# Reordering k conversions, two O units and one attention pair in a fused retention and feed-forward kernel

## The chip, the cores and the metric

One core of a Trainium2 chip. The metric is the time of one execution in microseconds (us), median over executions; lower is better. Each execution also has a span, from the first instruction of the program to the last, which the profiler gives to 0.1 us. All executions told here were in the fast state, except one of the kernel before (span 208.7 us), which is left out of every figure but the medians that the runs list and the count of 44 below. A ratio is the mean time of one kernel's fast runs over that of the kernel before's fast runs in the same rounds, so it is not quite the ratio of the medians that stand beside it.

## The reference

```python
def _attn_ref(q, k, v):                      # q, k, v: (4, 8, 768, 64)
    gamma = 1.0 - 2.0 ** (-5.0 - np.arange(H))
    for t in range(S):
        state = gamma * state + einsum('bhd,bhe->bhde', k[:, :, t], v[:, :, t])
        y[:, :, t] = scale * einsum('bhd,bhde->bhe', q[:, :, t], state)
def _moe_ref(x, w_in, w_out):                # x: y as (3072, 512)
    h = x @ w_in                             # (3072, 2048)
    return (h * np.cos(h)) @ w_out           # (3072, 512)
```

The sequence is cut into chunks of 128 steps. Twelve "pairs" (two batch entries, one chunk) go through attention; every two pairs make a group of 512 tokens that then goes through the two large products.

## The kernel before

Names used below: **A** is the score product of a pair (TensorE), masked by VectorE; **Y** is its output product, copied to `xt` by ScalarE, followed by **S**, the state product; **F** is a block of the first large product, ending in a cosine on ScalarE and a product on VectorE; **O** units (four matmuls) make the second large product. Pairs count from 0, so the "fourth pair" is pair 3 and the "seventh" pair 6. F (2,2) and F (3,0) are blocks of pairs 2 and 3 (`pair_f`); in the second half of the program F runs over whole groups, and F (2,11) is unit 11 of group 2. k is converted to bf16 by ScalarE (`conv_k`), q and v are converted by GpSimd (POOL), which also issues the loads. The program is one fixed order for each engine:

```python
    def conv_k(p, on_act, bs=(0, 1)):
        for b in bs:
            if on_act:
                nc.scalar.copy(out=qk[p % NB][:, b, 1], in_=kf[SLOT[p]][b])
    ...
    def act(bank, out):
        nc.scalar.activation(out=cb, in_=bank, func=AF.Sin, bias=halfpi)
        ...
        nc.vector.tensor_tensor(out=out, in0=bank, in1=cb, op=ALU.mult)
    ...
    cq(3)
    stage_t_dma(3)
    cv(3)
    load_both(("k", 4), ("q", 4), ("k", 5), ("q", 5), ("v", 4), ("v", 5))
    ...
    pair_f(2, 0)
    conv_k(4, True)
    pair_f(2, 1)
    attend(3)
    cq(4)
    stage_t_dma(4)
    pair_f(2, 2)
    conv_k(5, True)
    cq(5)
    ...
    pair_f(2, 3)
    stage_y(3, nc.scalar.copy)
    unit_o(1, 0, 0)
    pair_f(3, 0)
```

Seven PSUM banks rotate among A, Y, F and O. Which bank each takes is fixed when the program is built, by a small model of the engines' clocks.

## Time and profile before

| | before |
|---|---|
| median time, first three runs | 207.13 us |
| profiled execution: time, span | 207.53 us, 205.7 us |
| TensorE busy | 196.7 us, 96% |
| next engine (ACT) | 114.4 us, 56% |

How to read a line of the timeline: start, length, engine, source line, operation, output and input, number of merged instructions, and in brackets how long the engine had stood idle and what ended that. The lines themselves are in the prediction.

### The profile page before, as it was taken

The page shows a single profiled execution, that of the slowest core. Times are in us where ns is not written, and L with a number is a line of the kernel's source. Part 1 is how long each engine was busy: PE and PEld are TensorE (multiplying, and loading weights), DVE is VectorE, ACT ScalarE, POOL GpSimd, SP SyncE. Part 2 cuts the span into 40 slices and gives each one's busy share as a digit, 9 for nine tenths or more (in the row PEclk, how much of TensorE's full clock was granted, in tenths as well). Part 3 has the DMA queues.
Part 4 walks back from the last instruction along what each step waited for, and adds up shares of the span by engine and source line. Part 5 has one row for each costly group of instructions (what it writes and reads, how often), then busy time and mean ns, then how long its engine had stood idle before and what let it go on. Part 6 is the DMA issues. An engine that isn't in the chain of part 4 may idle for free.

```text
span 205.7 us, 4083 instructions
## 1 busy us (share of the span) xinstructions
PE 196.7 (96%) x1609; PEld 112.4 (55%) x1631; DVE 113.0 (55%) x190; ACT 114.4 (56%) x192; POOL 91.3 (44%) x98
## 2 busy tenths in 40 slices
PE   6789999999899999999999999999999999999993
PEld 2468544558797555556454466444465444444453
DVE  4886872723958545679784366844467233444000
ACT  7796862277885736597446466453554654553120
POOL 8998238399699659979931730000000000000000
PEclk9999999999999999999999999999999999999999
DMA  6999999959999995999999905101101101110212
GB/s 157 351 246 205 218 247 288 329 121 275 328 134 246 333 217 112 291 319 185 255 371 362 255 29 127 53 5 49 51 3 53 51 14 40 51 51 4 99 51 102
DMA packets 33571, 34.34 MB, mean 167 GB/s; under 512 B 23376, under 2 KB 25680, under 8 KB 33552
## 3 DMA queue, kind: packets, MB, share of 16 engines
q0 software_dynamic: 7824, 22.29, 38.9%
q1 hardware_dynamic: 24544, 11.44, 24.2%
q10 hardware_dynamic: 1184, 0.36, 0.7%
q8 instruction: 12, 0.20, 0.4%
q14 instruction: 7, 0.06, 0.1%
HBM read 27.26 MB, written 6.29 MB: 163 GB/s over the span
## 4 chain that ended last, share of the span: by engine, by line
PE 89%; DMA 2%; POOL 2%; DVE 2%; issue 2%; ACT 2%; ACTq 0%; POOLq 0%; DVEq 0%
PE bank L388 38%; PE bank L342 32%; PE bank L353 7%; PE bank L283 3%; PE bank L261 2%; DMA vf<-in_v_dram 2%; PE bank L288 2%; PE bank L366 2%; PE bank L408 2%; PE st_ps L305 1%; POOL qf L130 1%; DVE am L270 1%; ACT cosb L331 1%; POOL kf L137 1%; PE bank L232 0%
## 5 line engine op out<-in xcount | busy, mean ns | idle before, releaser
L335 DVE TENSOR_TENSOR gt<-bank,cosb 128x512 bf16<-128x512 f32 x96 | 65.0, 689 | 61.2 <-ACT cosb L331 61.0
L331 ACT ACTIVATE cosb<-bank,halfpi 128x512 bf16<-128x512 f32 x96 | 65.0, 688 | 51.1 <-PE bank L342 43.0
L388 PE MATMUL bank<-w_out_sb,gt 128*128 128x512 bf16 x357 | 88.2, 379 | 1.0 <-issue 0.5
L342 PE MATMUL bank<-xt,w_in 128*128 128x512 bf16 x294 | 74.1, 380 | 0.7 <-issue 0.4
L388 PEld LDWEIGHTS <-gt 128*128 128x128 bf16 x368 | 35.4, 98 | 41.0
L342 PEld LDWEIGHTS <-w_in 128*128 128x128 bf16 x304 | 33.7, 114 | 30.8
L270 DVE TENSOR_TENSOR am<-bank,mask 128x512 bf16<-128x512 f32 x48 | 30.4, 682 | 4.0 <-PE bank L261 3.9
L204 POOL TENSOR_TENSOR vs<-vf,gk 128x512 bf16<-128x512 f32 x21 | 21.4, 1042 | 10.3 <-DMA vf<-in_v_dram 8.8
L197 POOL TENSOR_TENSOR qk<-qf,gq 128x512 bf16<-128x512 f32 x18 | 18.4, 1040 | 9.6 <-DMA qf<-in_q_dram 3.1
L210 ACT CAST qk<-kf 128x512 bf16<-128x512 f32 x24 | 13.9, 618 | 14.1 <-DMA kf<-in_k_dram 13.9
L395 ACT COPY ob<-bank 128x512 f32<-128x512 f32 x23 | 13.4, 585 | 12.9 <-PE bank L388 12.6
L292 ACT CAST xt<-bank 128x512 bf16<-128x512 f32 x24 | 12.8, 591 | 5.9 <-PE bank L288 5.8
L353 PE MATMUL bank<-xt,w_in 128*128 128x256 bf16 x128 | 14.6, 273 | 0.8 <-DVE gt L335 0.7
L353 PEld LDWEIGHTS <-w_in 128*128 128x128 bf16 x128 | 13.9, 113 | 1.7 <-issue 1.2
L317 DVE CAST stb<-st_ps 64x512 bf16<-64x512 f32 x14 | 9.6, 686 | 3.6 <-PE st_ps L305 3.4
L288 PE MATMUL bank<-am,vs 128*64 128x128 bf16 x192 | 11.4, 220 | 0.0
L283 PEld LDWEIGHTS <-stb 128*64 128x64 bf16 x160 | 8.8, 109 | 4.0 <-issue 3.1
L283 PE MATMUL bank<-qkt,stb 128*64 128x128 bf16 x160 | 10.5, 222 | 0.3 <-ACT stb L317 0.3
L137 POOL DMA_DIRECT2D kf<-in_k_dram x9 | 10.5, 1168 | 0.0
L288 PEld LDWEIGHTS <-vs 128*64 128x64 bf16 x192 | 9.9, 110 | 0.5 <-issue 0.4
L137 POOL DMA_DIRECT2D qf<-in_q_dram x8 | 9.2, 1152 | 0.0
L137 POOL DMA_DIRECT2D vf<-in_v_dram x8 | 9.2, 1150 | 0.0
(47 smaller groups left out, 95.2 us busy)
## 6 DMA issues: line engine op xcount, KB each, us to landing
out_dram<-ob SPq DMA_DIRECT2D x23, 256.0 KB, 2.3
kf<-in_k_dram POOLq DMA_DIRECT2D x9, 512.0 KB, 6.1
qf<-in_q_dram POOLq DMA_DIRECT2D x8, 512.0 KB, 7.2
vf<-in_v_dram POOLq DMA_DIRECT2D x8, 512.0 KB, 8.2
vf<-in_v_dram POOLq DMA_DIRECT2D x8, 256.0 KB, 5.3
w_out_sb<-in_moe_w_out_dram POOLq DMA_DIRECT2D x4, 512.0 KB, 12.5
qf<-in_q_dram POOLq DMA_DIRECT2D x6, 256.0 KB, 7.1
w_in<-in_moe_w_in_dram POOLq DMA_DIRECT2D x3, 512.0 KB, 8.3
```

What stands on the lines that cost most here:

```text
L137: nc.gpsimd.dma_start(out=both[n][SLOT[p]].rearrange("p b h d -> p (b h) d"), in_=SRC[n][1][2 * bp : 2 * bp + 2, :, ds(c * C, C)].rearrang ...
L197: eng.tensor_tensor(out=qk[p % NB][:, b, 0], in0=qf[SLOT[p]][b], in1=bc(gq, p % NC), op=ALU.mult)
L204: eng.tensor_tensor(out=vs[p % NB][:, b], in0=vf[SLOT[p]][b], in1=bc(gk, p % NC), op=ALU.mult)
L210: nc.scalar.copy(out=qk[p % NB][:, b, 1], in_=kf[SLOT[p]][b])
L270: nc.vector.tensor_tensor(out=am[p % 2][b][j], in0=ap[j], in1=mask.unsqueeze(1).to_broadcast([128, HP, 128]), op=ALU.mult)
L283: nc.tensor.matmul(yp[ts(j, 64), a, :], lhsT=stb[p % 2][j][:, b, a, :], rhs=qt(n, b, a), start=True, stop=False, skip_group_check=True)
L288: nc.tensor.matmul(yp[ts(j, 64), a, :], lhsT=vs[n][:, b, 2 * a + j, :], rhs=am[p % 2][b][j][:, a, :], start=(c == 0), stop=True, skip_grou ...
L331: nc.scalar.activation(out=cb, in_=bank, func=AF.Sin, bias=halfpi)
L335: nc.vector.tensor_tensor(out=out, in0=bank, in1=cb, op=ALU.mult)
L342: nc.tensor.matmul(bank, lhsT=w_in_t(i, f), rhs=xt[g % 2][:, i, :], start=(i == 0), stop=(i == KIN - 1))
L353: nc.tensor.matmul(bank[:, ts(e, 256)], lhsT=w_in_t(i, f + e), rhs=xt[g % 2][:, i, ts(hf, 256)], start=(i == 0 and e == 0), stop=(i == KIN ...
L388: nc.tensor.matmul(bank, lhsT=gt[g % 2][:, f, ts(j, 128)], rhs=w_out_sb[:, f, :], start=(f == 0), stop=(f == KOUT - 1))
```

## The change

Its intent: no conversion of k should stand in ScalarE's queue before its data has landed, TensorE should have work behind Y of pair 3 while `xt` is copied, and pair 6 should fit the earlier arrival.

```diff
     pair_f(2, 0)
+    pair_f(2, 1)
     conv_k(4, True)
-    pair_f(2, 1)
     attend(3)
 ...
     pair_f(2, 2)
+    pair_f(2, 3)
+    stage_y(3)
     conv_k(5, True)
 ...
-    pair_f(2, 3)
-    stage_y(3, nc.scalar.copy)
     unit_o(1, 0, 0)
+    unit_o(1, 0, 1)
     pair_f(3, 0)
 ...
-    o_units(1, 1, 2)
+    o_units(1, 2, 3)
     conv_k(6, True)
     attend(4)
-    o_units(1, 2, 6)
+    o_units(1, 3, 6)
 ...
-    k_at = {(2, 4): 8, (2, 7): 9, (3, 5): 10, (3, 12): 11}
+    k_at = {(2, 6): 8, (2, 8): 9, (3, 5): 10, (3, 12): 11}
-    a_at = {(2, 2): 6, (2, 10): 7, (3, 2): 8}
-    y_at = {(2, 6): 6, (2, 14): 7, (4, 14): 11}
+    a_at = {(2, 3): 6, (2, 10): 7, (3, 2): 8}
+    y_at = {(2, 7): 6, (2, 14): 7, (4, 14): 11}
```

I call the first hunk part 1, the next three part 2 (Y and two O units ahead of `conv_k(5)`), and the last part 3.

## The prediction

> **What bounds the kernel now.** I read the page first, then the busy time by stretch, then the waits of TensorE (PE), and last the order of instructions from 46 to 58 us, engine by engine. The page and its slices:
>
> ```profile
> PE 196.7 (96%) x1609; PEld 112.4 (55%) x1631; DVE 113.0 (55%) x190; ACT 114.4 (56%) x192; POOL 91.3 (44%) x98
> ...
> PE   6789999999899999999999999999999999999993
> ...
> PEclk9999999999999999999999999999999999999999
> ```
>
> PE is busy for 196.7 of 205.7 us at the full clock; no other engine passes 56%. So the change, which issues exactly the same matmuls, copies and transfers, can only win the time in which PE stands still. Where is that? Busy time of each engine by stretch (us; columns: stretch, its length, PE, weight loads, DVE, ACT, POOL, then clock and DMA):
>
> ```profile
> 0.00:15.17 15.17, 11.69 (x159) 6.56 (x161) 10.82 (x33) 11.96 (x27) 14.23 (x22) 1.00 0.96 252
> 15.17:44.00 28.83, 28.64 (x206) 16.44 (x211) 18.45 (x28) 15.20 (x25) 17.11 (x21) 1.00 1.05 247
> 44.00:58.00 14.00, 12.87 (x166) 10.90 (x163) 7.46 (x12) 12.08 (x22) 11.82 (x12) 1.00 0.91 244
> 58.00:76.30 18.30, 18.04 (x206) 12.69 (x207) 11.79 (x18) 10.99 (x18) 14.41 (x15) 1.00 1.14 245
> 76.30:104.00 27.70, 27.42 (x235) 14.70 (x237) 19.60 (x32) 17.71 (x29) 25.64 (x24) 1.00 0.92 236
> 104.00:202.70 98.70, 98.00 (x656) 51.10 (x664) 44.51 (x69) 46.46 (x73) 8.13 (x8) 1.00 0.28 88
> ```
>
> Start (3.5 us idle) and end (3 us) aren't touched by the diff. From 58 us on PE lacks 1.2 us in 145, and these are small holes where a matmul is missing from the records (fewer matmuls than weight loads in the same column). Only 44 to 58 us has real holes, 1.13 us, and all touched stretches up to 104 us have nothing else to give. What PE did there, and what its neighbours did:
>
> ```profile
> 50.10 1.06 PE L353 MATMUL bank<-xt,w_in 128*128 128x256 bf16 x8
> 51.89 2.78 PE L353 MATMUL bank<-xt,w_in 128*128 128x256 bf16 x24 [0.72 <-DVE gt L335]
> ...
> 56.09 0.81 PE L388 MATMUL bank<-w_out_sb,gt 128*128 128x512 bf16 x3 [0.16 <-issue]
> 56.99 7.15 PE L353 MATMUL bank<-xt,w_in 128*128 128x256 bf16 x64
> ```
>
> ```profile
> 47.97 0.69 ACT L331 ACTIVATE cosb<-bank,halfpi 128x512 bf16<-128x512 f32 x1 [0.20 <-PE bank L353]
> 49.38 1.14 ACT L210 CAST qk<-kf 128x512 bf16<-128x512 f32 x2 [0.73 <-DMA kf<-in_k_dram]
> 50.43 1.83 ACT L331 ACTIVATE cosb<-bank,halfpi 128x512 bf16<-128x512 f32 x3
> ```
>
> The k conversion of pair 4 stands in ScalarE's queue before the cosines of F block 1. k landed at 44.17 + 5.2 = 49.4 us, so the cosine whose bank was full at 48.8 started at 50.43, VectorE's product ran 51.14 to 51.83, and PE, wanting that PSUM bank, resumed at 51.89.
>
> **What the Trainium skill says.** (1) "PSUM — Partial Sum Buffer", Engine vs sequencer instructions: ScalarE's and VectorE's queues are strict FIFO. The lines above agree: a full bank waited 1.6 us behind a conversion without data. (2) "TensorE: Matmul & The Clock Gate", Wait — 56ns, not 53.3ns?: a warm matmul is issued every N / 2.4 GHz + 2.5 ns, which I work out as 109 ns for 256 columns and 216 ns for 512. The chain agrees: 32 of 256 columns in 3.51 us (110 ns), 4 of 512 in 0.86 us (215 ns). (3) "Perfetto Trace Analysis", Matmuls (under Optimizing Tensor Performance): groups should rotate through banks so that evacuation overlaps the next group. Here seven banks rotate, and the hole comes exactly where rotation runs out. (4) "DMA: Bandwidth & Descriptors", Anatomy of one DMA: about 2.0 us plus bytes/436e3 per DMA, so 3.2 us for these 512 KB. The trace has 5.2 to 8.4 us (several in flight), and the trace counts.
>
> **The change part by part.** Nothing is added or removed except that pair 3's state copy goes from ACT (2 x 0.58 us) to DVE (2 x 0.69 us). The rest is order.
>
> *conv_k(4) behind F block (2,1).* Its cosines then run as soon as PE is done: about 48.84 and 49.71 instead of 50.43 and later. Product of the first: 49.55 to 50.25. PE reaches the second bank of F (2,2) at 50.10 + 8 x 0.110 = 50.98, and the bank is free. Hole removed: 51.89 - 50.98 = 0.91 us. (The profile's 0.72 counts from the modelled end of the last matmul.) k of pair 4 has landed (49.4) before its conversion, now at about 50.4.
>
> *F (2,3) and Y of pair 3 before conv_k(5), and two O units behind Y.* Weight loads show the one O unit started at 55.86, so its four matmuls ended issuing at 55.87 + 0.86 = 56.73; F (3,0) started at 56.99, when ACT's second xt copy ended (55.87 + 1.07 = 56.94). Hole: 0.25 us. Now Y's copies no longer stand behind 1.14 us of conversion: F (2,3) ends at about 53.6, Y at 54.95, copies at about 54.4 to 55.5, then conv_k(5) to 56.65. Two O units last to 54.95 + 1.73 = 56.68, 1.2 us after the copies. Hole gone with room. The second unit is only moved from after F (3,3), so it costs nothing.
>
> *Pair 6's A and Y, and conv_k(8), conv_k(9) later.* PE has no hole between 76.3 and 104 us, so nothing is to be won. They compensate: PE arrives there 1.16 us sooner, while loads are issued by POOL on its own schedule. ACT waits 1.21 us for k of pair 8 (lands 80.12 + 5.0 = 85.1) today without PE noticing. Moved to unit (2,6), its conversion starts about 85.3, just after landing.
>
> Sum: 0.91 + 0.25 = 1.16 us, if nothing downstream takes it back.
>
> Checks of what could: masks of pair 3 on DVE run 51.1 to 53.6, first two needed at 53.6 (done 52.4), last at 54.1. A of pair 4 at 64.5 needs transposes that landed by 62.1 (54.62 + 7.5). Its masks end at 67.7; Y of pair 4 now starts 67.9, and its second half needs the last mask at 68.4: 0.7 us left. A of pair 5 at 69.1 takes the bank of the first O result, which ACT copies behind conv_k(6): k lands 61.30 + 5.5 = 66.85, conversion to 68.0, copy to 68.5: 0.6 us left. A of pair 6 at 79.6, Y at 85.4: v of pair 6 is converted by 76.2. Around 88 to 91.6 us ACT is the tightest: xt copies, cosines, conv_k(9), an O copy. I estimate 0.1 us of PE waiting before F unit 11, since its bank frees at about 91.5 to 91.7 and PE comes at 91.6. Net gain: 1.16 - 0.1 = about 1.05 us.
>
> **The rivals.** *A. Loads get later.* If POOL's q conversion of pair 5 waited for conv_k(5), which ends 1.84 us later (56.65 against 54.81), then the fetch of pairs 6 and 7 would too, k of pair 6 would land at 68.7, the O copy would end at 70.4, and A of pair 5 would stall 1.2 us: the whole gain gone, 207.1 to 207.4. For it: conversions write two parts of one tile. Against: every q conversion starts within 0.2 us of its own q landing (45.36 + 6.8 = 52.16, start 52.21; 47.64 + 7.5 = 55.1, start 55.30; 62.49 + 5.9 = 68.4, start 68.47; 83.59 + 6.9 = 90.5, start 90.59), and pair 3's first half started at 39.67 while the second half of its k conversion began at 40.29. One chance in eight.
>
> *B. The wait moves into the seven banks.* ACT is denser after 85 us, so cosines lag and units 9 to 11 wait: up to 0.6 us back, 206.6. I count 0.1 of it. One chance in six for the larger size.
>
> *C. The hole is smaller in the timed runs.* The profiled run took 207.53 us, the median 207.13. If k lands earlier there, less is won: 206.3 to 206.5.
>
> **Range and chances.** Median 207.13 - 1.05 = 206.1 us. PE's holes cap the gain at about 1.2 us, so 205.5, allowing for run noise (before: 206.99 to 207.72) is the low end; rivals A to C set the high end at 206.9. Two per cent is 4.1 us, more than three times everything movable: within 2% is almost certain.
>
> **What would show it.** Right: PE's wait for DVE's product before L353 at 51.9 gone; ACT's waits for k of pairs 4 and 8 gone or under 0.2 us, while pair 6's stays and grows from 1.99 to about 2.3 us (the F blocks before it end 0.3 us sooner); F (3,0) following O with no hole; PE busy about 197 in a span of 204.6; POOL's fetches at 61.3 and 80.1 unmoved. Wrong: fetches about 1.8 us later and a PE wait at L261 near 69 (rival A); PE waits before L342 at 88 to 93 us (rival B); or a wait of Y for masks near 54 or 68.

## The result, and the profile after

Median 206.76 us (206.51 to 207.08, 6 runs) against 207.24 us of the kernel before in the same rounds; ratio 0.997, interval 0.9946 to 0.9994: within 2%, and a small gain. The profiled execution took 206.72 us, with a span of 204.7 us against 205.7.

The page of the kernel after, its row of engines:

```profile
PE 196.3 (96%) x1609; PEld 112.5 (55%) x1631; DVE 114.6 (56%) x192; ACT 113.6 (55%) x190; POOL 91.4 (45%) x98
```

The same work, two state copies moved from ACT to DVE. Busy time by stretch (columns as before):

```profile
44.00:58.00 14.00, 13.68 (x174) 11.56 (x171) 8.83 (x14) 11.46 (x21) 12.62 (x13) 1.00 0.94 245
58.00:76.30 18.30, 18.04 (x205) 12.63 (x206) 11.78 (x18) 10.74 (x19) 13.67 (x14) 1.00 1.05 244
76.30:104.00 27.70, 27.42 (x235) 14.69 (x237) 20.96 (x33) 17.84 (x30) 25.66 (x24) 1.00 0.95 234
```

TensorE's idle time between 44 and 58 us fell from 1.13 to 0.32 us, and two of the holes left are missing records of 0.16 us each. The two later stretches are as they were. Now the timeline of TensorE, then of ScalarE, in the same part:

```profile
50.15 3.69 PE L353 MATMUL bank<-xt,w_in 128*128 128x256 bf16 x32
...
55.26 1.67 PE L388 MATMUL bank<-w_out_sb,gt 128*128 128x512 bf16 x7 [0.16 <-issue]
56.77 7.15 PE L353 MATMUL bank<-xt,w_in 128*128 128x256 bf16 x64
```

```profile
49.76 0.69 ACT L331 ACTIVATE cosb<-bank,halfpi 128x512 bf16<-128x512 f32 x1 [0.19 <-PE bank L353]
50.35 1.13 ACT L210 CAST qk<-kf 128x512 bf16<-128x512 f32 x2
51.38 1.43 ACT L331 ACTIVATE cosb<-bank,halfpi 128x512 bf16<-128x512 f32 x2
...
54.50 1.06 ACT L292 CAST xt<-bank 128x512 bf16<-128x512 f32 x2
55.45 1.16 ACT L210 CAST qk<-kf 128x512 bf16<-128x512 f32 x2
```

For comparison, ScalarE of the kernel before, where the `xt` copies stand behind `conv_k(5)` and two cosines:

```profile
53.67 1.14 ACT L210 CAST qk<-kf 128x512 bf16<-128x512 f32 x2
...
55.87 1.07 ACT L292 CAST xt<-bank 128x512 bf16<-128x512 f32 x2
```

All 32 matmuls of F (2,2) and F (2,3) now run in one piece: the stop at 51.89 is gone. `conv_k(4)` has no idle time in front of it. The `xt` copies end at 55.56, while the O units last until 56.77, where F (3,0) follows without a hole. The last O block of the program (L408) starts at 197.91 in place of 199.00 us: 1.09 us sooner, although this execution had reached 46 us 0.05 us later. So the trace shows 1.14 us of holes closed and nothing given back. Yet the median of the times moved by only 0.48 us. The experiments are about that difference, and about which part does what.

### The profile page after: what moved, and what is told of

The parts are those of the page before. It is cut to its first block, busy times and chain, and to the rows that moved or that the text cites. A ratio compares the mean times of both kernels' runs of the same rounds, so it can differ in the third digit from the quotient of the medians.

```text
span 204.7 us, 4084 instructions
## 1 busy us (share of the span) xinstructions
PE 196.3 (96%) x1609; PEld 112.5 (55%) x1631; DVE 114.6 (56%) x192; ACT 113.6 (55%) x190; POOL 91.4 (45%) x98
## 4 chain that ended last, share of the span: by engine, by line
PE 91%; DVE 4%; DMA 2%; issue 1%; ACT 0%; DVEq 0%
PE bank L388 39%; PE bank L342 32%; PE bank L353 7%; PE bank L283 3%; PE bank L261 3%; PE bank L288 2%; PE bank L366 2%; DVE am L270 2%; DMA qf<-in_q_dram 2%; PE bank L408 2%; PE st_ps L305 1%; DVE qk L197 1%; DVE qkt L216 1%; PE bank L232 1%; ACT stb L317 0%
## 5 line engine op out<-in xcount | busy, mean ns | idle before, releaser
L317 DVE CAST stb<-st_ps 64x512 bf16<-64x512 f32 x16 | 11.0, 685 | 2.8 <-PE st_ps L305 2.5
```

## The experiments

All kernels gave correct results. Twelve runs, five rounds each and one profiled execution. Spans (us) are sorted:

| run | median time | before, same session | ratio | spans of the six executions |
|---|---|---|---|---|
| changed kernel, first | 206.76 | 207.24 | 0.9970 | 204.6 204.6 204.6 204.7 204.8 204.8 |
| e1_k4_later | 207.25 | 207.79 | 0.9988 | 205.0 205.1 205.2 205.5 205.6 206.7 |
| e2_y3_first | 208.22 | 207.79 | 1.0013 | 205.1 205.2 206.1 206.4 206.5 207.2 |
| e3_pair6_later | 207.41 | 207.79 | 0.9993 | 205.3 205.4 205.6 205.7 205.7 206.5 |
| e4_after_pair6_back | 207.57 | 207.79 | 0.9995 | 204.8 204.9 205.6 205.6 205.7 206.5 |
| e5_after_again | 206.87 | 207.65 | 0.9976 | 204.8 204.8 204.8 204.9 205.0 206.7 |
| e6_before_slow_pe | 208.44 | 207.65 | 1.0035 | 206.5 206.5 206.6 206.7 206.7 206.9 |
| e7_after_slow_pe | 208.34 | 207.65 | 1.0031 | 206.4 206.4 206.4 206.5 206.6 207.0 |
| e8_k4_fetched_sooner | 207.05 | 207.65 | 0.9967 | 204.9 205.1 205.1 205.2 205.3 205.4 |
| e9_one_o_unit | 207.03 | 207.51 | 0.9976 | 204.6 204.7 204.7 205.0 205.6 206.4 |
| e10_pair6_back_again | 207.18 | 207.51 | 0.9980 | 204.7 204.8 205.1 205.8 206.4 206.6 |
| e11_more_warm | 206.81 | 207.51 | 0.9981 | 204.6 204.7 204.8 204.8 204.9 206.1 |
| e12_pair6_back_third | 206.99 | 207.33 | 0.9973 | 204.7 204.8 204.9 205.0 205.1 205.6 |

The kernel before ran 44 times beside these: 36 spans from 205.2 to 206.1 (mean 205.60, called early below), then none up to 206.5, seven from 206.5 to 207.3 (late), and the slow one of 208.7. Only e6, e7 (slower, by the added work), e8 and the first comparison have an interval clear of 1; the rest is read from the profiles and the spans.

e5 is the changed kernel once more. Expected before it ran: spans of 204.6 to 204.9 us in early executions and about 206.4 in late ones, and a gain of the median time of 0.4 to 1.0 us; the rival was a fixed gain of 1.05 us with no span above 205.2. Measured: five spans of 204.8 to 205.0, one of 206.7, and a gain of 0.78 us. The rival is out.

**A rival in the build.** A new order could also change which PSUM bank each product takes. When the small model of the engines' clocks is run out of each kernel's own text, the kernel before, the changed one, e1 and e8 take the same banks up to the start of F (3,0), and e8 takes those of the kernel before in the whole program. So neither hole was closed by other banks.

**The two kinds of start.** Every profile with a span of 206.4 or more and no added work (e2, e4, e5, e10) shows the same thing, and none of the ten others does. Transposes of the first and second half of pair 0, TensorE's timeline of the kernel before, then of e5:

```profile
5.09 0.75 PE L232 MATMUL bank<-ident,qk 128*128 128x128 bf16 x8 [0.38 <-DVE qk L197]
...
7.41 0.85 PE L232 MATMUL bank<-ident,qk 128*128 128x128 bf16 x8
```

```profile
5.48 1.03 PE L232 MATMUL bank<-ident,qk 128*128 128x128 bf16 x8 [0.69 <-DVE qk L197]
...
8.67 1.02 PE L232 MATMUL bank<-ident,qk 128*128 128x128 bf16 x8
```

The same eight transposes take 1.03 us, and again 1.02 us at 8.67. By the view of lines one of them lasts 307 ns on average, against 221 in the kernel before (what lengthens its 0.75 and 0.85 us is a pause after the fourth). By the starts of single matmuls in the traces, TensorE is fast from 5.1 us at the latest in the kernel before, from 5.8 to 7.0 in e1, e9 and e12, and only from 9.5 to 10.7 us in the four late profiles. The Trainium skill, "TensorE: Matmul & The Clock Gate", What's actually happening, says that the array starts at half its clock and is released after a busy window of about 3.4 us, and that the window runs freely. The steps here, which wander from execution to execution, fit it; that this is their cause is not shown, since the profile's row of the granted clock stays at 1.00 throughout. In a late start TensorE reaches pair 2's first F block at 47.8 to 48.0 us in place of 46.0: 1.8 to 2.0 us late, without any change of the code before that point. The loads are late by less: k of pair 4 is fetched at 44.55 to 44.81 us, against 43.86 to 44.57 in the early profiles that leave its place alone.

### Part 1 alone

```diff
     pair_f(2, 0)
-    conv_k(4, True)
     pair_f(2, 1)
+    conv_k(4, True)
```

> Kernel before with conv_k(4) alone moved behind F block (2,1). Theory 1 (the two holes are chained through the queue of ScalarE): the 0.91 us hole before the second bank of F (2,2) goes, but ScalarE then stands at conv_k(5) until k of pair 5 lands (about 53.7), and F (3,0) can't start before that plus conversion 1.14, two cosines 1.26 and two xt copies 1.07, so about 57.1: the hole before F (3,0) grows from 0.25 to about 1.3 us. Gain of the span 0.0 (-0.2 to +0.2). Rival (the parts add up as in the prediction): gain 0.9 us, hole before F (3,0) stays at 0.25.

Measured: the hole at F (2,2) is gone, and the hole before F (3,0) is 0.35 us: S starts at 54.71, the O unit runs from 55.06 to 55.92, and F (3,0) starts at 56.27. ScalarE and TensorE in e1:

```profile
52.95 1.14 ACT L210 CAST qk<-kf 128x512 bf16<-128x512 f32 x2
54.00 1.26 ACT L331 ACTIVATE cosb<-bank,halfpi 128x512 bf16<-128x512 f32 x2
55.15 1.07 ACT L292 CAST xt<-bank 128x512 bf16<-128x512 f32 x2
```

```profile
56.27 7.15 PE L353 MATMUL bank<-xt,w_in 128*128 128x256 bf16 x64 [0.17 <-ACT xt L292]
```

The chain that I named is there: conversion, two cosines, two copies, then F (3,0). But k of pair 5 landed at 46.63 + 6.3 = 52.9 us here, not at 53.7, so the chain ended sooner. The five early spans average 205.28, a gain of 0.3 us against 205.60: neither theory's number. The landing time of a load, which I had taken as fixed, moves by 0.8 us between executions.

### Part 2 alone

```diff
     pair_f(2, 2)
-    conv_k(5, True)
+    pair_f(2, 3)
+    stage_y(3)
+    conv_k(5, True)
 ...
-    pair_f(2, 3)
-    stage_y(3, nc.scalar.copy)
     unit_o(1, 0, 0)
+    unit_o(1, 0, 1)
```

(with the counts of the following `o_units` calls changed as in the whole change)

> Kernel before with Y of pair 3 and F (2,3) ahead of conv_k(5), state copy on VectorE and the second O unit behind Y; conv_k(4) and pairs 6, 8, 9 as before. Both theories: the hole at F (2,2) stays at about 0.9 us, the one before F (3,0) goes, gain of the span about 0.25 us. Theory 1 says that this with e1 is worth more than the two alone (1.1 against 0.25).

Measured: at least three of the six executions, the profiled one among them, started late; the two early ones have spans of 205.1 and 205.2, which is 0.45 us under the mean of before. Two executions are too few for a size, and for a test of Theory 1: 0.3 us of e1 and 0.45 us here add up to nearly the gain of the whole change, which speaks for parts that add up, not for a chain. Whether the first hole stays in an early execution of e2 no profile shows. The late profile taught more than the expected one would have: `conv_k(4)` stands in its old place, yet its 32 matmuls of F (2,2) and (2,3) take 3.73 us in one piece. TensorE came 1.75 us later, so k had landed, and there was no hole to close.

### Part 3 alone

```diff
-    k_at = {(2, 4): 8, (2, 7): 9, (3, 5): 10, (3, 12): 11}
+    k_at = {(2, 6): 8, (2, 8): 9, (3, 5): 10, (3, 12): 11}
```

(and A and Y of pair 6 one unit later, as in the whole change)

> Kernel before with only conv_k(8), conv_k(9), A and Y of pair 6 moved later. Theory 1: ScalarE's wait for k of pair 8 (1.21 us) goes, TensorE had no hole there, so the span stays within 0.15 us. Rival (a ScalarE wait costs time wherever it is): 0.5 to 1.2 us faster.

Measured: spans as the kernel before's (five early ones, mean 205.54). ScalarE no longer waits for k of pair 8. So part 3 wins nothing by itself, as predicted. Its profile shows how much the holes vary, since the code up to 76 us is that of the kernel before. Its TensorE timeline:

```profile
50.11 1.06 PE L353 MATMUL bank<-xt,w_in 128*128 128x256 bf16 x8
51.59 2.78 PE L353 MATMUL bank<-xt,w_in 128*128 128x256 bf16 x24 [0.41 <-DVE gt L335]
```

By the prediction's own count, the first hole is 51.59 - (50.11 + 8 x 0.110) = 0.60 us in place of 0.91; the second is 0.13 in place of 0.25. k of pair 4 was issued 0.17 us sooner and took 5.1 in place of 5.2 us.

### A later TensorE, in both kernels

```diff
+    slow = banks.take()
+    for _ in range(8):
+        nc.tensor.matmul(slow, lhsT=ident, rhs=xt[0][:, 0, :], start=True, stop=True,
+                         skip_group_check=True)
+    banks.give(slow, clk.pe)
     pair_f(2, 0)
```

> Kernel before with eight idle matmuls of 512 columns (8 x 0.216 = 1.73 us) put on TensorE just ahead of F block (2,0), loads untouched. Theory: k of pair 4 has landed by the time ScalarE reaches its conversion, so the hole at F (2,2) shrinks to about 0.1 us and the kernel gets slower by only 0.8 to 1.3 us. Rival (the hole is fixed work of the order, not lateness of a load): slower by 1.6 to 1.9 us.

> Changed kernel with the same eight idle matmuls at the same place. Both theories: nothing is hidden there, so it gets slower by the whole 1.6 to 1.8 us against the changed kernel. By the theory the two slowed kernels then differ by only 0.2 to 0.5 us; by the rival by about 1.0 us.

Measured: 1.73 us of idle matmuls made the kernel before slower by 206.65 - 205.60 = 1.05 us (median span against the early mean), and the changed kernel by 206.45 - 204.8 = 1.65 us. The median spans of the slowed kernels differ by 0.2 us, their mean spans and median times by 0.1. TensorE of e6:

```profile
52.06 3.73 PE L353 MATMUL bank<-xt,w_in 128*128 128x256 bf16 x32
```

3.73 us for the 32 matmuls against 3.69 in the changed kernel: a hole of 0.04 us. This run and e8 below settle the cause of the first hole: nothing in the order of ScalarE was touched, and a later TensorE removed it. (The idle matmuls shift the rotation of the banks by one, which e8 does not.) The second hole is still there in e6: the O unit starts at 56.99, its four matmuls of 0.215 take it to 57.86, and F (3,0) starts at 57.99, 0.13 us later, although k of pair 5 had landed at 46.60 + 6.5 = 53.1 us, 1.6 us before its conversion started. The pair of runs imitates a late start: with TensorE late by 1.73 us the change is worth 0.1 to 0.2 us, not 0.84. Real late starts are too few to say: the changed kernel has one, of 206.7, and the two of the kernel before in the same session have 207.2 and 207.3.

### k of pair 4 fetched sooner

```diff
     stage_t_dma(3)
+    load_both(("k", 4))
     cv(3)
-    load_both(("k", 4), ("q", 4), ("k", 5), ("q", 5), ("v", 4), ("v", 5))
+    load_both(("q", 4), ("k", 5), ("q", 5), ("v", 4), ("v", 5))
```

> Kernel before with order of ScalarE untouched, but k of pair 4 fetched ahead of the v conversion of pair 3 on POOL, so 2.0 us sooner (landing about 47.4). Theory: ScalarE's wait for it goes and the hole at F (2,2) falls to 0.1 to 0.2 us (the conversion itself still stands before the cosine); F (3,0) still waits for the xt copies behind conv_k(5), so its hole is 0.2 to 1.0 us, and the gain of the span is 0.2 to 0.7 us. Rival (the conversion's place in the queue costs, whatever its data): hole at F (2,2) stays above 0.4 us.

Measured: median span 205.15, so 0.45 us under the early mean of before, ratio 0.9967 (0.9941 to 0.9993). ScalarE and TensorE of e8:

```profile
48.66 1.13 ACT L210 CAST qk<-kf 128x512 bf16<-128x512 f32 x2
49.69 1.27 ACT L331 ACTIVATE cosb<-bank,halfpi 128x512 bf16<-128x512 f32 x2
```

```profile
50.21 3.73 PE L353 MATMUL bank<-xt,w_in 128*128 128x256 bf16 x32
```

The conversion stands where it stood, ahead of the cosines, and no longer waits; the hole is 0.04 us. So what cost TensorE at the first hole was the landing of the load; the 1.13 us of conversion just fit into the slack. The second hole is still there, at 0.13 us, and again `conv_k(5)` did not wait for its data (landed at 46.51 + 5.6 = 52.1 us, started at 52.82). So at the second hole the conversion's own length, ahead of the cosines and copies, costs something.

### One O unit behind Y

```diff
     unit_o(1, 0, 0)
-    unit_o(1, 0, 1)
     pair_f(3, 0)
```

(and the unit back behind F (3,3))

> Changed kernel with the second O unit back behind F (3,3), so only one behind Y of pair 3. Theory: Y's copies end at about 55.55 while one O unit lasts until about 55.8, so F (3,0) starts without a hole and the second unit is spare: span as the changed kernel, 204.6 to 204.9 us, hole before F (3,0) under 0.1. Rival (the second unit is what closes the hole of 0.25 us): slower by 0.2 to 0.3 us, hole of 0.2 to 0.3 before F (3,0).

Measured: in the profile (span 204.7) the one O unit starts at 55.06, four matmuls of 0.215 take it to 55.92, and F (3,0) starts at 55.93:

```profile
55.06 1.04 PE L388 MATMUL bank<-w_out_sb,gt 128*128 128x512 bf16 x4
55.93 7.15 PE L353 MATMUL bank<-xt,w_in 128*128 128x256 bf16 x64
```

The hole is closed without the second unit. Moving Y's copies ahead of `conv_k(5)` closed it; the second O unit is a margin.

### The third part undone, three times

```diff
-    k_at = {(2, 6): 8, (2, 8): 9, (3, 5): 10, (3, 12): 11}
+    k_at = {(2, 4): 8, (2, 7): 9, (3, 5): 10, (3, 12): 11}
```

(changed kernel; A and Y of pair 6 back as well)

> Changed kernel with conv_k(8), conv_k(9), A and Y of pair 6 back at their old units. Theory 1: TensorE now arrives about 1.1 us sooner, k of pair 8 still lands at about 85.1, so ScalarE waits about 2.4 to 3.1 us there in place of 1.2, cosines lag, and TensorE stalls for a bank near A of pair 7 (about 91 us) by 0.3 to 1.0 us: part of the gain is given back. Rival (the third part is idle): same span as the changed kernel within 0.15 us.

> The same kernel as the changed one with the third part undone, once more, since its profile before fell on a late start and its spans went from 204.8 to 206.5. Theory: in an early start ScalarE waits for k of pair 8 by 2 us or more and TensorE then stalls 0.3 to 1.0 us between 86 and 92 us in part of the executions (span about 205.6), in others not (204.8). Rival (the third part is idle and 205.6 was chance): spans 204.6 to 204.9 as the changed kernel.

> Third look at the changed kernel with its third part undone; both profiles so far fell on a late start (span 206.5, 206.6), in which ScalarE's wait for k of pair 8 is only 0.5 to 1.2 us and TensorE doesn't notice. Theory: in an early start that wait is 2 us or more, and the executions at 205.6 to 205.8 us (4 of 12 so far, against 0 of 12 of the changed kernel) are those in which TensorE stalls 0.5 to 1.0 us for it between 85 and 92 us. Rival: no stall there in an early start either, span 204.6 to 205.0 in the profile, and the 205.6 to 205.8 executions come from partly cold starts.

Measured: the first two profiles fell on late starts and show nothing of it. The third is an early one, with a span of 204.8. ScalarE of e12:

```profile
84.48 1.14 ACT L210 CAST qk<-kf 128x512 bf16<-128x512 f32 x2 [1.74 <-DMA kf<-in_k_dram]
```

ScalarE waits 1.74 us, its cosines lag until about 91 us, and the masks of pair 7 on VectorE end at 95.45 in place of 95.28. From the start of F (2,11) to S of pair 7 TensorE took 95.94 - 91.28 = 4.66 us, against 95.78 - 91.27 = 4.51 in the changed kernel, and A of pair 7 takes 0.68 in place of 0.62. Together that is some 0.2 us lost, with k of pair 8 landing by 84.5 us, sooner than the 85.1 of the kernel before. My expectation of 0.3 to 1.0 us was not met in this execution. Over all, 5 of 18 executions without the third part lie at 205.6 to 205.8, and none of 12 of the changed kernel does (one of six of e9, which has the third part, lies at 205.6). That a later landing makes these is likely, since the slack is used up in the one profile, but no profile shows it: it stays open.

### Nine idle matmuls at the start

```diff
-    warm(8)
+    warm(9)
```

> Changed kernel with nine idle matmuls at the start in place of eight, to fill the 0.3 to 0.7 us in which TensorE stands before the first transposes. Theory: executions that start cold (matmuls at half rate until about 10.4 us, span about 206.5) get fewer; no span of the six above 205.3, median 204.6 to 204.9. Rival (cold starts have another cause): one or two of six spans at 206 or more, median unchanged.

Measured: five spans of 204.6 to 204.9 and one of 206.1. The filled gap is in the profile, but a span of 206.1 is what the rival forecast, and the changed kernel itself gives one late span in twelve, so six executions show no fewer late starts. Inconclusive, and no gain. No run here has shorter spans than the changed kernel.

## Why the prediction was right or wrong

**Right: where the time is.** Only the two holes between 44 and 58 us were to be had. Their idle time fell by 0.81 us in the view by stretch, and the last block of the program starts 1.14 us sooner once the 0.05 us of the front are counted; I had worked out 1.16. That the prediction's 1.13 us of idle time came so close to 1.16 is chance: 0.32 of it is two missing records, which stand in the profile after too, and the view counts idle time from modelled ends.

**Right: the cause of the first hole.** A conversion without data in front of a cosine, in a queue that runs in order. e8 and e6 remove the lateness by two other ways, and the hole goes to 0.04 us in both.

**Right: the cause of the second hole**, Y's copies behind `conv_k(5)` and its cosines: with the copies ahead it is gone (e9, with one O unit as before). The second O unit was not needed.

**Right: part 3 wins nothing itself** (e3). That it protects the gain is supported by the 0.2 us that e12 lost without it, not more.

**Right: rival A is out.** POOL of the kernel after:

```profile
54.52 2.04 POOL L197 TENSOR_TENSOR qk<-qf,gq 128x512 bf16<-128x512 f32 x2 [1.06 <-PE bank L288]
...
60.70 1.19 POOL L137 DMA_DIRECT2D kf<-in_k_dram  x1
```

q of pair 5 is converted from 54.52, before ScalarE even starts `conv_k(5)` at 55.45, and the fetch follows at 60.70, not at 63. The bracket names a matmul of Y, but q of pair 5 itself landed at 47.66 + 6.7 = 54.4 us, 0.2 us before the conversion.

**Right: rival B is out.** F (2,11) starts at 91.27, 0.55 us after A of pair 7, the same distance as before (91.84 to 92.39): the 0.1 us that I had set aside was not lost.

**Wrong in a detail:** ScalarE's wait for k of pair 6 did not grow to 2.3 us; it fell to 1.24, since the fetch came 0.6 us sooner (60.70 in place of 61.30), behind a q of pair 5 that landed sooner. The prediction had held this fetch to be unmoved.

**Wrong in size: the step from the holes to the median.** The text says "Median 207.13 - 1.05 = 206.1 us". The measured median, 206.76, lies in the range, but by only 0.14 us at its high end, which the rivals had set; the gain in time is 0.48 us in that session and 207.65 - 206.87 = 0.78 in the second, not 1.05. The 1.16 us of holes were read in an execution of 207.53 us and subtracted from a median of 207.13. From the same execution it would have been 207.53 - 1.05 = 206.48. Rival C said just this ("the hole is smaller in the timed runs") and I gave it too little weight: e3 shows holes of 0.60 + 0.13 = 0.73 us in an execution of span 205.3, and over many executions the early spans fall by 205.60 - 204.76 = 0.84 us (36 of 44 of the kernel before, 11 of 12 of the changed one). In five profiles the span less the holes is nearly the same: 204.54 in the kernel before (205.7 - 1.16), 204.57 in e3, 204.75 in e1, 204.73 in e8, and 204.7 in the changed kernel, which suggests that the early spans of the kernel before vary with their holes. The remaining 0.3 us between 206.48 and 206.76 is outside the program's span: time less span was 1.8 to 2.5 us in the six executions of the changed kernel, 1.83 in the profiled one of before. What makes that difference vary is open.

**Missed: the late start.** It appears nowhere in the prediction. In it TensorE is late by 1.8 to 2.0 us, the loads by some 0.5, so the first hole is hidden (e2). With TensorE made late on purpose the change is worth 0.1 to 0.2 us (e6 against e7); how much in a real late start stays open.

## What to carry to other kernels

Put an instruction that waits for a load behind the work in its engine's queue that others wait for, and check by the issue and landing times whether the load or the instruction's own length is what costs: at the first hole it was the load, at the second 0.13 us remained although the data had landed (e6, e8). When holes are to be subtracted from a time, subtract them from the execution in which they were read, and ask whether a late load and a late engine can hide each other, since then the gain depends on how the program started. A change of half a per cent is read from spans and traces of the same kind of start, not from six times.

## What the Trainium skill lacked or had wrong

- "DMA: Bandwidth & Descriptors", Anatomy of one DMA, gives one transfer alone, which for 512 KB makes an estimate of 3.2 us. With several in flight the same size took 4.9 to 9.4 us here between 44 and 86 us, and one and the same load (k of pair 5, order of loads unchanged) 5.9 to 7.2 us between executions; the page has no figure for either.
- "TensorE: Matmul & The Clock Gate", Wait — 56ns, not 53.3ns? agrees: 215 ns for 512 columns and 110 ns for 256.
- The same page, What's actually happening, calls the slow matmuls at the start variable from run to run and their penalty less than 1% of a typical kernel's span. That agrees: 1.8 to 2.0 us at 46 us, in spans of 205 to 207. What it lacks is that this is more than a change such as this one is worth, so that runs must be sorted by their start, and that the profile's clock row can stay at 1.00 all the while.
- No page has the 1.7 to 3.6 us between the program's span and the measured time, or why it varies ("Runtime: NRT & Kernel Launch" has a gap between another pair of times).
